# A second buffer for the keys of a head pair, loaded at an earlier place in the DMA queue

## The chip, the core and the metric

The kernel runs on one core of a Trainium2 chip. The metric is the device time in microseconds (us) of one execution, from its first to its last instruction and what lies around them. A core has a tensor engine (TensorE; PE in the profile, with its weight loads as PEld), a vector engine (DVE), a scalar engine (ACT), a GpSimd engine (POOL) and a sync engine (SP). Here SP computes nothing: nearly all DMA transfers are issued from its queue, in order, and an instruction that has to wait holds up all those behind it.

## The reference

Attention with queries that are averaged in pairs, for 8 batches of 8 heads, 1152 keys of 64 numbers, so 576 pooled queries per head; its output, put together as 576 rows of 512 per batch, goes through a token and channel mixing stage. All inputs and the output are float32.

```python
q_pool = q.reshape(B, H, S // 2, 2, D).mean(axis=3)
scores = scale * np.matmul(q_pool, k.transpose(0, 1, 3, 2))
attn = np.exp(scores - np.max(scores, axis=-1, keepdims=True))
attn = attn / (np.sum(attn, axis=-1, keepdims=True) + 1e-09)
x = np.matmul(attn, v)            # then (B, 576, 512)
theta = x @ w_theta
y = einsum('ts,bsd->btd', w_tok_r, x * cos(theta)) + einsum('ts,bsd->btd', w_tok_i, x * sin(theta))
u = x + y
out = u + np.maximum(u @ w_ch, 0.0)
```

## The kernel before

**Two stages.** The first computes the attention for 32 pairs of heads, one pair after the other; the second computes the mixing for the 8 batches. The change touches the first alone.

**Precision.** Each float32 operand of the scores is split into a rounded part `hi` and a rest `lo`, and a tile of scores is the sum of three products of these and of a fourth product that subtracts the maximum of each query (`escore`, L365). So before a pair's scores can start, its queries and keys must be transposed and split (`prep_t`, `prep_hi`, `prep_lo`), and the maxima of its scores must be known (`maxpass`, `max_tail`, `max_nm`). The maxima come as a tile with 9 rows (`mT`); four small DMAs bring them into one row per head (`load_max`, L358).

**The order.** The order is written out by hand: `plan(i)` (L643) puts every step of pair i at a position, 18 positions to a pair, position 18 i being the pair's first score tile. All steps of all pairs are sorted by position (L690) and issued in that order, and each engine and the DMA queue then goes through its own instructions in that order. In the stretch of a pair n (positions 18 n to 18 n + 18) lie

- the 18 score tiles of pair n (two halves of the queries, u = 0 and 1, with nine key blocks each), with the exponentials on ACT and the adds of the denominators on POOL (`ssum`, L387; 14 per pair);
- the 12 maxima passes of pair n + 2, one every position or two, each with two matmuls and a DVE reduction;
- at position 10.35 `burst(n, 0)`: the second part of the transposes of pair n + 2 (queries and the last three key blocks, `prep_t(n + 2, 1)`), the 36 matmuls with the values for u = 0 (`av`), and the transpose of the maxima of pair n + 1 into `mT`;
- at position 10.4 `load_max(n + 1)`, at 10.79 `load_k(n + 3)`, at 11 `load_v(n + 1)` and the store of the denominators, all on the queue of SP;
- at position 19.27, that is 1.27 positions into the next pair, `burst(n, 1)`: `tail_prep(n)` with the first part of the transposes of pair n + 3 (six key blocks, `prep_t(n + 3, 0)`) and the last maxima pass of pair n + 2, and then the `av` matmuls for u = 1.

So the keys of a pair are read twice: the first six blocks at the end of the pair three before it, the last three blocks nine positions later. The tile `kn` of a pair has one buffer (pool `inp`, `bufs=1`), and the load of the next pair's keys into it has to come after the second reading.

**Banks.** All TensorE results of this stage go in turn through four PSUM double banks (`bank2("e", ...)`, `PAIRS`): a tile can be written once the tile four before it has been read by ACT or DVE.

**Weights.** Beside the attention the weights of the second stage are loaded and split in pairs 0 to 17, one job to a pair, in small steps on DVE, POOL and ACT (`weights`, `W_SLOTS`): among them two DVE operations (L524, L528) after `burst(n, 1)`, then two POOL operations (L530, L532) that need them, and for the token weights five transposes on TensorE (L574, L581) just ahead of `burst(n, 0)`.

The lines that set the positions and issue the keys:

```python
at(base + pl["load_q"], 5, load_q, i)      # L646, base = 18 * i
at(base + pl["load_k"], 5, load_k, i)      # L648
kn = inp.tile([P, KT, 2, D], F32, tag="kn", name=f"kn{i}")                      # L226
nc.sync.dma_start(kn[:, :, h, :], k[b, h0 + h].rearrange("(p t) d -> p t d", t=KT))  # L228, h = 0, 1
```

Of the kernel before, what the change touches and what calls it, by code (L numbers as in the profile page):

```python
# [9 lines left out]
F32 = mybir.dt.float32  # L10
# [16 lines left out]
MAX_AT1 = (-18.123, -16.8, -16.1, -15.375, -14.7, -14.0, -13.3, -12.6, -11.714, -10.295, -9.8, -8.999)  # L27
PLAN = {
    "load_q": -44.542,
    "load_k": -43.209,  # L30
    "pool_q": -35.622,
    "load_max": -7.6,
    "load_v": -7.0,
# [41 lines left out]
def pooled_attention_moe_kernel(  # L75
# [12 lines left out]
    P = 128  # L88
    B, H, S, D = k.shape
# [5 lines left out]
    KT = S // P  # L95
# [94 lines left out]
    with ExitStack() as p1:  # L190
# [4 lines left out]
        inp = p1.enter_context(tc.tile_pool(name="inp", bufs=1))  # L195
# [16 lines left out]
        state = {}  # L212

        def load_q(i):
            b, hp = divmod(i, NP)
            h0 = 2 * hp
            qn = inp.tile([QP, 2, QT, 2, D], F32, tag="qn", name=f"qn{i}")
            nc.sync.dma_start(
                qn, q[b, h0 : h0 + 2].rearrange("h (p t f) d -> p h t f d", t=QT, f=2)
            )  # L220
            state[i] = dict(qn=qn)

        def load_k(i):
            b, hp = divmod(i, NP)
            h0 = 2 * hp
            kn = inp.tile([P, KT, 2, D], F32, tag="kn", name=f"kn{i}")  # L226
            for h in range(2):
                nc.sync.dma_start(kn[:, :, h, :], k[b, h0 + h].rearrange("(p t) d -> p t d", t=KT))  # L228
            state[i]["kn"] = kn

        def pool_q(i):
            qn = state[i]["qn"]
# [410 lines left out]
        def plan(i):  # L643
            base = NU * i
            pl = PLAN
            at(base + pl["load_q"], 5, load_q, i)  # L646
            at(base + pl["pool_q"], 5, pool_q, i)
            at(base + pl["load_k"], 5, load_k, i)  # L648
            if i < 3:
                at(PRO[i][0], 3, prep_all, i, 0)  # L650
            if i < 2:
                at(PRO[i][1], 3, prep_all, i, 1)
                at(PRO[i][2], 3, lambda i=i: (max_tail(i, None), max_tail_red(i)))
            if i == 0:
                at(-7.62, 3, first_row)
            at(base + pl["load_max"], 7, load_max, i)
            at(base + pl["load_v"], 5, load_v, i)
            gen = maxpass(i)
            for n in (MAX_AT0, MAX_AT1, MAX_AT)[min(i, 2)]:
                at(base + n, 2, run, gen, 1)  # L660
            at(base + pl["max_nm"], 7, max_nm, i)
            for u in range(2):
                for kt in range(KT):
                    at(base + KT * u + kt, 1, escore, i, u, kt)
                    at(base + KT * u + kt + (SS_LAG if i < NPAIR - 1 else 1.2), 8, ssum, i, u, kt)
            for u in range(2):
                at(base + AV_AT[u], 4, burst, i, u)
            for n, fn in (
                ("norm_spread", norm_spread),
                ("norm_store", norm_store),  # L670
            ):
                at(base + pl[n], 9, fn, i)
# [316 lines left out]
```

## Time and profile before

| | |
|---|---|
| median of 3 runs | 1400.39 us (1399.51 to 1400.64) |
| the profiled execution | 1399.06 us |
| its span, first to last instruction | 1397.3 us |
| first stage (32 pairs), until the tail of the last pair | about 888 us |
| TensorE busy | 1324.2 us (95%), mean granted clock 0.992 |
| POOL busy | 957.4 us (69%) |
| DVE busy | 817.3 us (58%) |
| ACT busy | 726.4 us (52%) |
| DMA | 111.64 MB, mean 80 GB/s |

The profile shows one execution. A line of the timeline gives the start, the duration, the engine and the line of the kernel, the operation with the tile it writes and those it reads, and in brackets how long the engine was idle before it and what ended that. Matmuls are pipelined: their starts are recorded, their ends are modelled. The waits sum, for each engine and line, the idle time and name the event that came last before its end. Busy times by windows are sums over all instructions of a stretch.

### The profile page before, as it was taken

To read this page: it belongs to the slowest core of one execution; us is meant where nothing else is said; L and a number is where in the kernel's file an instruction comes from. 1 tells how busy PE (TensorE), PEld (TensorE's weight loads), DVE (VectorE), ACT (ScalarE), POOL (GpSimd) and SP (SyncE) were. 2 spreads that over 40 slices of the span, in tenths; PEclk is the share of its full clock that TensorE was granted. 3 is DMA by queue.
4 is the path that set the end of the run, shared out by engine and by line. 5 is a ranking of instruction groups with operands and counts; after the bars stand their busy time and mean duration, and the time that the engine had idled before them with its cause. 6 is when DMAs were issued, how large, how long until landed. Compare 5 with 4: busy or idle time off the path is not lost.

```text
span 1397.3 us, 29769 instructions
## 1 busy us (share of the span) xinstructions
PE 1324.2 (95%) x12178; PEld 1081.9 (77%) x12178; DVE 817.3 (58%) x1056; ACT 726.4 (52%) x1272; POOL 957.4 (69%) x727
## 2 busy tenths in 40 slices
PE   5999999999999999999999999879999999999998
PEld 4667777777777777767677777579999999999998
DVE  5677777777776876555465552656354453536442
ACT  2556566566656656556555555544453444445431
POOL 2799999999999999788788788463452624345220
PEclk9999999999999999999999999889999999999999
DMA  5334343433433333233233223141212122121111
GB/s 125 101 93 114 98 110 88 115 96 101 125 88 109 86 89 86 65 92 87 61 96 86 61 62 99 34 143 47 60 54 75 54 68 69 47 60 54 27 32 37
DMA packets 123992, 111.64 MB, mean 80 GB/s; under 512 B 88128, under 2 KB 88512, under 8 KB 123856
## 3 DMA queue, kind: packets, MB, share of 16 engines
q1 hardware_dynamic: 123680, 109.28, 28.1%
q8 instruction: 96, 1.57, 0.5%
q0 software_dynamic: 176, 0.46, 0.1%
q14 instruction: 40, 0.33, 0.1%
HBM read 88.29 MB, written 21.27 MB: 78 GB/s over the span
## 4 chain that ended last, share of the span: by engine, by line
PE 76%; DMA 9%; DVE 5%; ACT 4%; issue 2%; POOL 2%; SPq 1%; POOLq 0%; ACTq 0%; DVEq 0%
PE pa L403 20%; PE pe L382 17%; PE py L820 12%; DMA kn<-in_k_dram 8%; PE pth L748 7%; PE pr L859 6%; PE pt L267 4%; PE pm L307 3%; PE pn L424 2%; DVE mx L314 2%; PE pxn L736 1%; PE px L324 1%; POOL ss L394 1%; ACT pc L385 1%; ACT xh L724 1%
## 5 line engine op out<-in xcount | busy, mean ns | idle before, releaser
L394 POOL TENSOR_TENSOR ss<-ss,pc 128x576 f32<-128x576 f32 x384 | 552.9, 1440 | 85.7 <-ACT pc L385 61.5
L314 DVE TENSOR_REDUCE mx<-pm 128x2 f32<-128x768 f32 x384 | 355.5, 956 | 182.3 <-PE pm L307 181.7
L385 ACT ACTIVATE pc<-pe 128x576 f32<-128x576 f32 x576 | 353.9, 652 | 63.3 <-PE pe L382 42.8
L403 PE MATMUL pa<-pc,vn 128*64 128x288 f32 x2304 | 293.5, 409 | 0.0
L820 PE MATMUL py<-wtk,Z 128*128 128x288 f32 x1728 | 244.0, 298 | 6.9 <-DVE r L765 6.9
L403 PEld LDWEIGHTS pa<-pc,vn 128*64 128x64 f32 x2304 | 159.5, 137 | 109.5 <-issue 3.3
L820 PEld LDWEIGHTS py<-wtk,Z 128*128 128x128 f32 x1728 | 235.0, 190 | 8.7 <-DVE r L765 7.3
L795 POOL TENSOR_TENSOR Z<-ab,Z 128x512 fp32r<-128x512 f32 x40 | 52.1, 1302 | 269.5 <-ACT Z L791 220.3
L382 PE MATMUL pe<-hi 64*128 64x288 f32 x1152 | 198.1, 340 | 1.8 <-DVE mx L314 0.7
L382 PE MATMUL pe<-lo,hi 64*128 64x288 f32 x1152 | 170.4, 292 | 0.0
L382 PE MATMUL pe<-hi,lo 64*128 64x288 f32 x1152 | 170.2, 292 | 0.0
L382 PE MATMUL pe<-nmr,oner 64*128 64x288 f32 x1152 | 170.2, 292 | 0.0
L382 PEld LDWEIGHTS pe<-hi 64*128 64x128 f32 x1152 | 108.1, 184 | 58.2 <-issue 23.1
L307 PE MATMUL pm<-hi 64*128 64x384 f32 x768 | 134.1, 347 | 3.9 <-ACT hi L283 2.1
L413 ACT COPY xu<-pa 128x288 f32<-128x288 f32 x64 | 25.6, 400 | 166.9 <-PE pa L403 123.9
L382 PEld LDWEIGHTS pe<-lo,hi 64*128 64x128 f32 x1152 | 109.1, 186 | 0.0
L382 PEld LDWEIGHTS pe<-nmr,oner 64*128 64x128 f32 x1152 | 108.6, 185 | 0.0
L382 PEld LDWEIGHTS pe<-hi,lo 64*128 64x128 f32 x1152 | 108.6, 185 | 0.0
L859 PEld LDWEIGHTS pr<-us,wch 128*128 128x128 f32 x768 | 104.4, 188 | 2.1
L859 PE MATMUL pr<-us,wch 128*128 128x288 f32 x768 | 105.9, 296 | 0.0
L294 DVE TENSOR_TENSOR lo<-pt,hi 128x768 fp32r<-128x768 f32 x64 | 67.4, 1053 | 48.5 <-ACT hi L283 48.5
L394 POOL TENSOR_TENSOR ss<-pc,pc 128x576 f32<-128x576 f32 x64 | 93.4, 1460 | 3.4 <-ACT pc L385 3.4
(108 smaller groups left out, 1700.4 us busy)
## 6 DMA issues: line engine op xcount, KB each, us to landing
qn<-in_q_dram SPq DMA_DIRECT2D x32, 576.0 KB
kn<-in_k_dram SPq DMA_DIRECT2D x64, 288.0 KB
vn<-in_v_dram SPq DMA_DIRECT2D x32, 576.0 KB
xd<-xu SPq DMA_DIRECT2D x32, 288.0 KB
xT<-xd SPq DMA_DIRECT2D x8, 1152.0 KB
dn<-rd SPq DMA_DIRECT2D x64, 144.0 KB
out_dram<-on SPq DMA_DIRECT2D x23, 192.0 KB
out_dram<-on SPq DMA_DIRECT2D x23, 128.0 KB
```

The lines of the kernel that those rows point to most:

```text
L267: nc.tensor.transpose(out=pt[:, n, c : c + R], in_=src.rearrange("p h d -> p (h d)"), identity=ident[0:R, 0:R],)
L294: nc.vector.tensor_tensor(lo, src, hi.bitcast(F32), ALU.subtract)
L307: nc.tensor.matmul(pm[:, h, 0:W], hi[hs, Q0 + j * P : Q0 + (j + 1) * P], hi[hs, K0[3 * g] : K0[3 * g] + W], start=True, stop=True,)
L314: nc.vector.tensor_reduce(mx[:, j : j + 5 : 4, g : g + 1], pm[:, :, 0:W], AX.X, ALU.max)
L382: nc.tensor.matmul(pe[:, h, 0:HALF], w[hs], x[hs], start=(n == 0), stop=(n == 3))
L385: nc.scalar.activation(pcs[u, kt], pe[:, :, 0:HALF], AF.Exp, scale=SC)
L394: nc.gpsimd.tensor_tensor(st["ss", u], first, st["pc"][u, kt], ALU.add)
L403: nc.tensor.matmul(pa[hs, 0, 0:HALF], st["vn"][:, h, kt, :], st["pc"][u, kt][:, h, :], start=(kt == 0), stop=(kt == KT - 1),)
L748: nc.tensor.matmul(th, xs[:, c, j * P : (j + 1) * P], ws[:, c], start=(n == 0), stop=(n == 11))
L795: engine("zlo", b).tensor_tensor(Z[1], t, Z[0].bitcast(F32), ALU.subtract)
L820: nc.tensor.matmul(st["py", c, u][:, 0:HALF], Z[zi][:, c * P : (c + 1) * P], wtk[wi][:, kw, u * HALF : (u + 1) * HALF], start=(i == 0 and ...
L859: nc.tensor.matmul(pr[u][:, 0:HALF], wch[wi][:, c, e * P : (e + 1) * P], st["us", ui][:, c, u * HALF : (u + 1) * HALF], start=(n == 0), st ...
```

## The change

The load of a pair's keys moves from position 18 i - 43.209 to 18 i - 53.5. Seen from the pair n in whose stretch it falls, `load_k(n + 3)` is issued at position 0.5, after the first score tile of pair n, in place of position 10.79 after `load_max(n + 1)`. The tile `kn` gets two buffers, which is 4608 bytes more in each partition. As `load_k` of a pair now comes ahead of its `load_q`, both put their tile into the pair's state without making it anew.

```diff
 PLAN = {
     "load_q": -44.542,
-    "load_k": -43.209,
+    "load_k": -53.5,
     "pool_q": -35.622,
     "load_max": -7.6,
     "load_v": -7.0,
@@ load_q
-            state[i] = dict(qn=qn)
+            state.setdefault(i, {})["qn"] = qn
@@ load_k
-            kn = inp.tile([P, KT, 2, D], F32, tag="kn", name=f"kn{i}")
+            kn = inp.tile([P, KT, 2, D], F32, tag="kn", name=f"kn{i}", bufs=2)
             for h in range(2):
                 nc.sync.dma_start(kn[:, :, h, :], k[b, h0 + h].rearrange("(p t) d -> p t d", t=KT))
-            state[i]["kn"] = kn
+            state.setdefault(i, {})["kn"] = kn
```

## Rows read from the trace of the kernel before

**Rows 1.** Waits of TensorE, whole span: engine, line, waited for: us, times, longest
```profile
PE pt L267 <- DMA kn<-in_k_dram: 33.2, 25, 7.8
...
PE pt L267 <- DVE mx L314: 4.1, 4, 1.1
...
PE pt L267 <- issue: 0.6, 1, 0.6
```

**Rows 2.** Windows: length, busy PE, PEld, DVE, ACT, POOL, clock, DMA share, GB/s
```profile
59.83:545.15 485.32, 466.03 (x5020) 348.45 (x5022) 356.21 (x401) 295.24 (x530) 450.88 (x332) 1.00 0.37 101
545.15:834.98 289.83, 280.21 (x3032) 208.86 (x3032) 162.93 (x190) 162.04 (x286) 236.07 (x175) 1.00 0.28 77
```

**Rows 3.** Timeline of TensorE, end of one pair and middle of the next
```profile
191.36 0.33 PE L307 MATMUL pm<-hi 64*128 64x384 f32 x2
192.40 0.85 PE L267 MATMUL pt<-ident,kn 128*128 128x128 f32 x6 [0.71 <-DMA kn<-in_k_dram]
193.00 0.71 PE L324 MATMUL px<-hi,tail 128*128 128x512 f32 x3
...
204.62 0.34 PE L307 MATMUL pm<-hi 64*128 64x384 f32 x2
204.89 0.71 PE L267 MATMUL pt<-ident,qp 96*128 96x96 f32 x6
```

**Rows 4.** Timeline of the queue of SP in the same pair
```profile
186.81 0.55 SPq L363 DMA_DIRECT2D nmr<-mT  x1
187.46 1.40 SPq L228 DMA_DIRECT2D kn<-in_k_dram  x2
...
190.82 1.16 SPq L497 DMA_DIRECT2D raw<-in_moe_w_tok_r_dram  x2
198.76 0.34 SPq L479 DMA_DIRECT2D xd<-xu  x1
```

**Rows 5.** Timelines of TensorE and DVE at the ends of two other pairs
```profile
327.75 0.84 PE L267 MATMUL pt<-ident,kn 128*128 128x128 f32 x6 [1.03 <-DVE mx L314]
...
649.12 0.85 PE L267 MATMUL pt<-ident,kn 128*128 128x128 f32 x6 [0.59 <-DMA kn<-in_k_dram]
...
648.57 0.96 DVE L314 TENSOR_REDUCE mx<-pm 128x2 f32<-128x768 f32 x1 [0.32 <-PE pm L307]
```

**Rows 6.** Timelines of DVE and ACT, end of the pair of Rows 3
```profile
189.60 1.82 DVE L314 TENSOR_REDUCE mx<-pm 128x2 f32<-128x768 f32 x2 [0.27 <-PE pm L307]
...
191.12 1.19 ACT L385 ACTIVATE pc<-pe 128x576 f32<-128x576 f32 x2 [0.16 <-PE pe L382]
```

**Rows 7.** Waits of POOL, from 59.83 to 545.15, then from 545.15 to 834.98
```profile
POOL raw L530 <- DVE raw L528: 12.8, 18, 1.6
POOL ss L394 <- ACT pc L385: 6.1, 10, 0.8
...
POOL ss L394 <- ACT pc L385: 46.0, 22, 3.0
```

**Rows 8.** Timelines of POOL and TensorE, a pair with token weights
```profile
119.22 1.47 POOL L532 TENSOR_TENSOR ws<-wf,raw 128x576 f32<-128x576 f32 x1
...
123.98 0.66 PE L574 MATMUL pwt<-ident,ws 128*128 128x128 f32 x4
```

**Rows 9.** Lines L524 and L528 on DVE: count, ns min/median/max, first and last start
```profile
L524 DVE SCALAR_TENSOR_TENSOR wf<-raw,wf x18: 680/942/1997, 62.0 to 520.4; 128x512 uint32<-128x512 uint32 x8, 128x576 uint32<-128x576 uint32 x8, 64x576 uint32<-64x576 uint32 x2
...
L528 DVE TENSOR_SCALAR raw<-wf x18: 428/1516/1553, 62.7 to 521.3; 128x512 uint32<-128x512 uint32 x8, 128x576 uint32<-128x576 uint32 x8, 64x576 uint32<-64x576 uint32 x2
```

**Rows 10.** Timelines of SP, DVE and TensorE, first microseconds
```profile
0.75 0.38 SPq L218 DMA_DIRECT2D qn<-in_q_dram  x1
1.20 1.45 SPq L228 DMA_DIRECT2D kn<-in_k_dram  x2
...
5.38 1.02 DVE L236 TENSOR_TENSOR qp<-qn 96x384 f32<-96x384 f32 x2 [4.41 <-DMA qn<-in_q_dram]
...
7.83 1.51 PE L267 MATMUL pt<-ident,kn 128*128 128x128 f32 x6 [7.83 <-DMA kn<-in_k_dram]
```

## The prediction

> **What bounds the kernel now.** I read the waits of TensorE first. Over the whole span it has 30 waits ahead of the first transposes of a pair's keys (L267): 25 are put down to the load of `kn`, 4 to a DVE reduction and 1 to nothing, 33.2 + 4.1 + 0.6 = 37.9 us [rows 1]. The longest, 7.8 us, is the start of the kernel [rows 10]; the other 29 are one for each pair whose end prepares a later one, 30.1 us, 1.04 us each. Nothing else of weight holds TensorE in this stage: from 59.83 to 834.98 it is busy for 466.03 of 485.32 us and 280.21 of 289.83 us, so idle for 19.3 and 9.6 us, whatever the cause [rows 2], and those 29 waits, less the first, are that. So the stage is bound by TensorE and one gap to a pair.
>
> The four waits put down to DVE are the same thing. At 327.75 the transposes start after 1.03 us, like their neighbours; at 649.12 they start while the last reduction, 648.57 to 649.53, still runs [rows 5]. That reduction is therefore not what they need, and its end beside the start at 327.75 is a coincidence.
>
> Why the keys are late is in the DMA queue: their two issues at 187.46 stand right behind the last maxima row (186.81), which waits for the middle of the pair, and the transposes start at 192.40, 4.9 us after the first issue [rows 3, 4]. TensorE comes to them at about 191.6.
>
> **The change, part by part.** *The wait.* Where no load is awaited, a transpose starts 0.27 us after the start of the last maxima matmuls (204.62, 204.89); at the end of the pair it starts 1.04 us after them (191.36, 192.40) [rows 3]. So 0.77 us go where the wait says 0.71, as the modelled end of the matmul overlaps what would follow. For 29 pairs that is 30.1 + 29 x 0.06 = 31.9 us. All of it lies on the path, since TensorE has no other idle time to take it up.
>
> *The new place in the queue.* The two issues (1.40 us) now come after the first score of pair n. Of SP's queue they pass the four maxima rows, the query load, a weight store in some pairs and the store of `xd`. They come to stand between the weight load (190.82 to 191.98) and that store (198.76) [rows 4]. SP stands idle between these for 6.8 us, so 1.40 us there delay nothing, and the value load behind the maxima rows goes out 1.40 us earlier. Were the cover gone, the store would slip by 1.40 us, and nobody on TensorE's path reads it. The transfer took 4.9 us with the value load behind it; behind a weight load I give it up to 8. It is wanted one pair after 192.40, and a pair takes about 27 us (485.3 us for 18, [rows 2]), so about 19 us are to spare.
>
> *The added wait.* The second buffer comes free with the last three key blocks of the pair two before, whose transposes lie just after the middle of the preceding pair: a pair before 204.89, so at about 178.5 [rows 3], 13 us ahead of the new issue. Behind a load that did wait there would be the store of `xd`, the queries and the maxima rows; I cost it at nothing.
>
> *What is late next on TensorE.* The transposes need the bank of the tile four before, the second reduction of a pair of them that ends at 191.42 (189.60 + 1.82), 0.2 us before TensorE would come at 191.63; the last maxima pass (`px`, 0.60 us after the transposes) needs an exponential that ends at about 191.7, half of 191.12 to 192.31, and would come at 192.23 [rows 3, 6]. Both are in time, the first by little: a cost between 0 and, at 0.1 us a pair, 2.9 us. I take 0, the row's own end.
>
> *POOL.* This is the cover that matters. In the pairs with weight work (59.83 to 545.15) POOL waits 12.8 us for DVE's L528 and 6.1 us for exponentials, together 18.9 us in 485.3 [rows 7]; TensorE would save up to 19.3 us there [rows 2]. The two come out level, so POOL has no time left in these 18 pairs. After 545.15 it waits 46.0 us while TensorE saves 9.6: ample [rows 2, 7]. A POOL that falls behind costs nothing until something on TensorE meets it. The nearest such thing is the token weights: POOL's L532 ends at 120.69, the transposes of its result start at 123.98, 3.3 us later [rows 8]. Bounds: if POOL can use all 18.9 us, it falls behind by 0.4 us overall and by 1 to 3 us (an estimate) after a pair or two with a long wait, and costs 0. If the 12.8 us can't be used, it falls behind by 19.3 - 6.1 = 13.2 us, and 13.2 - 3.3 = 9.9 us come back as waits. I take 1.3 us, near the lower end, since a wait is time in which POOL only stood.
>
> L528, the operation that POOL waits for, takes from 428 to 1553 ns, and L524 from 680 to 1997 [rows 9]: their spread is far more than their three sizes explain. The Trainium skill, "SBUF — State Buffer", section "Who interferes with whom", says that a VectorE instruction with two SBUF inputs or in a two-port mode and a GpSimd instruction that reads SBUF exclude each other, the later one blocked until the first is done. The spread in this trace agrees. By that rule a POOL add moved into today's waits would meet those two operations, the waits would come back as blocked time, and the sum would be the one with 9.9 us lost; it is the first rival.
>
> *The start.* Pair 0 now loads its keys ahead of its queries, and the keys of pair 1 follow at once. Today the queries are there at 5.38 and the keys at 7.83, 1152 KB after the first issues at 0.75 and 1.20 [rows 10]. Then the queries are the last, at about 7.8; their sums take 1.02 us on DVE, while the key transposes (1.3 us) are already done. That is 0.4 us better to, if the next 576 KB share the engines evenly at the 174 KB/us of these rows, 2.9 us worse. I take +0.2 us, as the queries that were issued first also landed first.
>
> *The sum.* From the profiled 1399.06 us: - 31.9 + 0.2 + 1.3 = - 30.4, so 1368.7. The median of the runs lies 1.3 us above the profiled one, which gives **1370.0 us**. The second stage starts after the last pair's sums and moves with them.
>
> **The rivals.** *POOL takes TensorE's place in the weight pairs.* For it: the level sums above, and the spread of L528. Against it: POOL's wait is idle time, and the lag has 3.3 us to grow. Time: 1399.06 - 31.9 + 0.2 + 9.9 + 1.3 = 1378.6.
>
> *Another wait takes the place of the load's,* at the bank or at the exponentials. For it: the margin of 0.2 us. Against: both are read to be in time. Were half the gap to stay, 16 us would be gained, 1384.
>
> *It doesn't do what it says:* the load is held in SP's queue until its old place. Against it: the buffer is free 13 us earlier. It would give the old time, 1399 to 1401.
>
> *Slower: POOL is displaced by DVE throughout.* A denser TensorE lets L524 and L528 always fall on POOL's adds, for their full medians, 0.94 + 1.52 = 2.46 us a pair, 44 us in 18 pairs [rows 9]. POOL would then need 485.3 - 18.9 + 44 = 510.7 us for the weight pairs, 25.4 more than they take now. Less the 9.6 us of the later pairs, and 2 of the pair before 59.83, it ends near 1414. It turns slower from a displacement of (18.9 + 9.6 + 2) / 18 = 1.7 us a pair. Against it: part of the 2.46 us is in today's times already, as the medians show.
>
> **How the numbers follow.** Chances: the forecast, 1366 to 1375, 0.66; POOL in TensorE's place, 1375 to 1385, 0.20; another wait, 1380 to 1395, 0.05; no effect 0.04; slower 0.05. The low end is 1366: no loss to POOL, 0.4 us won at the start, and some 2 us for waits that the trace puts elsewhere. The high end is 1381: the 1378.6 of the first rival with most of the start's 2.9 us. A difference under 0.2% (2.8 us) can't be told from none by a measurement of this kernel. Faster has the first three cases and comes to 0.91, same 0.04, slower 0.05.
>
> **What the profile after would show.** If the steps hold: the waits of L267 for `kn` are down to the one at the start; the two issues of `kn` stand between a weight load and the store of `xd`; TensorE is busy over 99% of the stretch of the pairs; POOL's waits in the weight pairs are nearly gone, those in the later pairs are down by some 10 us. The first rival would show waits of TensorE for POOL (at L574) or of ACT for buffers that POOL holds, and weight pairs longer by half a microsecond than their TensorE work. The second would show waits of L267 or L324 for DVE or ACT near 0.5 us. The prediction is wrong if the waits for `kn` go and the pairs still don't get shorter by about a microsecond.

## The result and the profile after

The changed kernel takes 1377.17 us (median of 4 runs, 1376.94 to 1378.85), against 1400.52 us for the kernel before beside it: a ratio of 0.9828 [0.9808, 0.9847], so faster by 1.7%. The measured gain is 23 us, where 30 were forecast (1370.0). The range of 1366 to 1381 holds the time, but only by the part that it has from the first rival: the time lies 2 us above the forecast's own case (1366 to 1375) and within 1.5 us of that rival's 1378.6.

The profiled run of the changed kernel took 1378.85 us (span 1377.1), 1.7 us above its median; that of the kernel before took 1399.06, 1.3 us below its median. The rows add up to the 20.2 us between these two.

**The waits of TensorE.** First those of the whole span, against [rows 1]; the columns are those of [rows 1].

```profile
PE pt L267 <- DMA kn<-in_k_dram: 7.2, 1, 7.2
...
PE pm L307 <- ACT pc L385: 5.1, 7, 0.8
...
PE pt L267 <- DVE qp L236: 2.5, 1, 2.5
```

Of the 30 waits for the keys one is left, that of the first pair. Two waits are new: 7 of the maxima matmuls for ACT's exponentials, all in the pairs with weight work, and one for the first pair's queries.

**Stretches of the same work.** I cut both profiles at the starts of the first key transposes at pair ends, as what lies between two such starts is the same work in both. Windows of the kernel before, then of the changed one: the 18 pairs with weight work, and the pairs after them up to the last such transposes. The columns are those of [rows 2].

```profile
58.46:543.77 485.31, 466.02 (x5018) 348.45 (x5019) 356.21 (x400) 295.24 (x530) 450.87 (x331) 1.00 0.37 101
543.77:808.72 264.95, 255.32 (x2761) 190.45 (x2761) 148.18 (x172) 147.29 (x260) 216.33 (x162) 1.00 0.30 80
```

```profile
57.08:529.92 472.84, 466.43 (x5020) 348.28 (x5019) 369.15 (x400) 296.79 (x531) 456.24 (x332) 1.00 0.41 105
529.92:785.37 255.45, 255.22 (x2762) 190.39 (x2760) 148.18 (x172) 147.19 (x261) 217.19 (x162) 1.00 0.31 83
```

The later pairs lose all their idle time: 264.95 to 255.45, beside 255.22 of TensorE's work. The pairs with weight work don't: 485.31 to 472.84, with 6.4 us of TensorE's time (472.84 - 466.43) still idle. All in all the gain is 2.8 us between the transposes of pair 0 (35.59 to 58.46 before, 37.01 to 57.08 now), 12.5 us, 9.5 us, less 1.4 us that the start takes longer (35.59 to 37.01), less 3.1 us in what follows the last transposes (588.6 before, 591.7 now).

**POOL and ACT in the pairs with weight work.** Waits of POOL in the changed kernel, from 57.08 to 529.92, and after the "..." from 529.92 to 785.37; then those of ACT for POOL in the first of these stretches.

```profile
POOL raw L530 <- DVE raw L528: 0.4, 1, 0.4
...
POOL ss L394 <- ACT pc L385: 30.1, 11, 3.3
```

```profile
ACT hl L541 <- POOL ws L532: 3.1, 4, 0.9
ACT wth L541 <- POOL ws L532: 2.8, 3, 0.9
ACT ws L514 <- POOL hl L543: 0.9, 4, 0.2
ACT ws L514 <- POOL wth L543: 0.6, 3, 0.2
```

POOL's 18.9 us of waits [rows 7] are down to 0.4: it is the engine that is full now. Who meets it is ACT, at the copy of a square weight (L541), 7 times for 5.9 us. ACT's exponentials are queued behind that copy, and TensorE waits for those: 7 times, 5.1 us. The timelines of POOL, ACT and TensorE show one such place, in the changed kernel:

```profile
170.32 1.31 POOL L532 TENSOR_TENSOR ws<-wf,raw 128x512 f32<-128x512 f32 x1
...
171.66 0.62 ACT L541 CAST wth<-ws 128x512 fp32r<-128x512 f32 x1 [0.92 <-POOL ws L532]
...
172.88 0.44 PE L307 MATMUL pm<-hi 64*128 64x384 f32 x2 [0.81 <-ACT pc L385]
```

The same step in the kernel before, in the pair with the least to spare:

```profile
199.81 1.31 POOL L532 TENSOR_TENSOR ws<-wf,raw 128x512 f32<-128x512 f32 x1
...
201.69 0.61 ACT L541 CAST hl<-ws 128x512 fp32r<-128x512 f32 x1
```

There POOL is done at 201.12 (199.81 + 1.31) and ACT comes at 201.69. ACT had no wait, but it had only 0.57 us to spare, and no row of waits shows a margin. At the other seven places where ACT makes this copy the margin before was 0.99 to 2.08 us.

**The queue.** The timeline of SP's queue shows the load where the prediction put it, between a weight load and the store of `xd`, with free time on both sides (in this pair a load of `rc` goes just ahead of it):

```profile
158.44 0.38 SPq L497 DMA_DIRECT2D raw<-in_moe_w_ch_dram  x1
161.22 0.34 SPq L161 DMA_DIRECT2D rc<-sd  x1
161.66 1.39 SPq L228 DMA_DIRECT2D kn<-in_k_dram  x2
167.70 0.33 SPq L479 DMA_DIRECT2D xd<-xu  x1
```

**The start.** First microseconds of the changed kernel, timelines of SP, DVE and TensorE:

```profile
0.76 1.48 SPq L228 DMA_DIRECT2D kn<-in_k_dram  x2
2.28 1.18 SPq L218 DMA_DIRECT2D qn<-in_q_dram  x1
3.50 1.96 SPq L228 DMA_DIRECT2D kn<-in_k_dram  x2
...
10.21 1.02 DVE L236 TENSOR_TENSOR qp<-qn 96x384 f32<-96x384 f32 x2 [9.24 <-DMA qn<-in_q_dram]
11.29 1.22 PE L267 MATMUL pt<-ident,qp 96*128 96x96 f32 x6 [2.54 <-DVE qp L236]
```

The queries of pair 0, issued second now, are there at 10.21 and not at 5.38 [rows 10], with the keys of the next pair issued behind them. This varies: in the four other profiled runs with these two buffers and this order they are there at 8.92 to 9.63.

### The profile page after: what moved, and what is told of

Same layout as the page of the kernel before. It is cut to its first block, busy times and chain, and to the rows that moved or that the text cites. A ratio compares the mean times of both kernels' runs of the same rounds, so it can differ in the third digit from the quotient of the medians.

```text
span 1377.1 us, 29805 instructions
## 1 busy us (share of the span) xinstructions
PE 1325.8 (96%) x12178; PEld 1081.0 (78%) x12178; DVE 830.6 (60%) x1056; ACT 727.7 (53%) x1272; POOL 961.5 (70%) x727
## 4 chain that ended last, share of the span: by engine, by line
PE 84%; DVE 5%; ACT 5%; POOL 3%; issue 2%; DMA 1%; SPq 0%; POOLq 0%; ACTq 0%; DVEq 0%
PE pe L382 23%; PE pa L403 20%; PE py L820 13%; PE pth L748 8%; PE pr L859 6%; PE pm L307 4%; PE pt L267 4%; PE pn L424 2%; DVE mx L314 1%; PE pxn L736 1%; POOL ss L394 1%; PE px L324 1%; ACT pc L385 1%; ACT xh L724 1%; PE po L882 1%
## 5 line engine op out<-in xcount | busy, mean ns | idle before, releaser
L394 POOL TENSOR_TENSOR ss<-ss,pc 128x576 f32<-128x576 f32 x384 | 560.2, 1459 | 68.2 <-ACT pc L385 42.0
L748 PE MATMUL pth<-wth,xh 128*128 128x512 f32 x320 | 93.4, 414 | 0.0
```

The lines of the kernel that those rows point to most:

```text
L394: nc.gpsimd.tensor_tensor(st["ss", u], first, st["pc"][u, kt], ALU.add)
L748: nc.tensor.matmul(th, xs[:, c, j * P : (j + 1) * P], ws[:, c], start=(n == 0), stop=(n == 11))
```

## The experiments

**Which half of the change does it?** The theory was that the place ahead of the maxima rows brings the gain and that the buffer only permits it. Two kernels take one half each, and a third has one buffer at another early place.

The second buffer alone, with the load at its old place:

```diff
-    "load_k": -53.5,
+    "load_k": -43.209,
```

> The second buffer alone: the keys are loaded at their old position 10.79, behind the maxima rows. Theory (the gain comes from the place in the queue, not from the buffer): the load is still held behind the maxima rows, so TensorE waits for the keys in 29 pairs as before, some 30 us, and the time is that of the kernel before, 1400 us, within 2 us. Rival (the single buffer held the load back, so that the second one is what gains): a gain of 10 us or more.

Measured: 1400.07 us, a ratio of 0.9986 [0.9970, 1.0002]. The waits of TensorE, whole span:

```profile
PE pt L267 <- DMA kn<-in_k_dram: 39.1, 29, 7.8
```

The waits are all there. The buffer by itself is worth nothing, since the keys were late by their place in the queue.

The new place alone, with one buffer:

```diff
-            kn = inp.tile([P, KT, 2, D], F32, tag="kn", name=f"kn{i}", bufs=2)
+            kn = inp.tile([P, KT, 2, D], F32, tag="kn", name=f"kn{i}")
```

> The new place alone, with the single buffer: the load stands at position 0.5 of SP's queue and waits there for the transposes at 10.35 of the same pair. Theory (place, not buffer, brings the gain, and the added wait costs only what stands behind it in the queue): the keys' issue falls just after those transposes, some 5 us ahead of the maxima rows and some 12 us ahead of its use, so the 29 waits for the keys go as in the changed kernel; the store of x and the loads of queries and weights behind it go out up to 13 us later, which has spare time for the queries: 1375 to 1382 us. Rival (the held queue makes something else late: weight loads, the maxima rows or the queries): TensorE waits elsewhere, 1385 to 1410 us.

Measured: 1390.20 us, 0.9922 [0.9904, 0.9940], 12.9 us above a second measurement of the changed kernel on the same chip (1377.27, below). The pairs are as in the changed kernel; the loss is at the start, where the first transposes of a pair end come at 41.76 us (35.59 before) and those of pair 0's end at 70.35 (57.08 in the changed kernel). The waits of TensorE and of SP's queue, whole span:

```profile
PE pm L307 <- ACT hi L283: 6.9, 3, 4.8
...
PE pe L382 <- DMA nmr<-mT: 4.9, 1, 4.9
```

```profile
SPq L228 <- PE pt L267: 470.1, 31, 16.8
```

The load now waits in the queue for the transposes that free its only buffer, about 15 us each time. In a pair SP has that time. At the start it hasn't: the first maxima rows are queued behind the load (issued from 31.23, 25.89 before). So the rival's cause was real, and the time lies in its range, but it acts at the start alone and not in every pair; the 29 waits for the keys went, as the theory said.

One buffer, and the load right behind the transposes that free it, so that nothing is held up in the queue (an edit of the kernel before):

```diff
-    "load_k": -43.209,
+    "load_k": -43.645,
```

> One buffer, the load at position 10.355: just behind the transposes that free it, ahead of the maxima rows, with nothing held in the queue; the first loads stay in their old order. Theory (the wait of the old place was for the maxima rows ahead of it alone): the issue falls some 5 us earlier than in the kernel before, the keys land some 4 us ahead of their use, all 29 waits go, and the time is that of the changed kernel less what that loses at the start, 1374 to 1376 us. Rival (the key transfer now lies ahead of the maxima rows on the DMA engines and makes them late): TensorE waits at the first scores of a pair, 1385 us or more.

Measured: 1378.21 us, 0.9832 [0.9818, 0.9847]; the pairs with weight work take 472.6 us. The waits of TensorE, and the first maxima row in the timelines of SP and TensorE:

```profile
PE pt L267 <- DMA kn<-in_k_dram: 7.8, 1, 7.8
```

```profile
28.44 1.31 SPq L228 DMA_DIRECT2D kn<-in_k_dram  x2
29.81 1.22 SPq L362 DMA_DIRECT2D nmr<-mT  x1
...
33.60 0.95 PE L382 MATMUL pe<-nmr,oner 64*128 64x288 f32 x2 [2.73 <-DMA nmr<-mT]
```

The 29 waits go with one buffer as well. The time came out 2 us over what was expected, as the keys of pair 2 go out just ahead of the first maxima row, for which TensorE stands 2.73 us; the first transposes of a pair end come at 39.86 us, 2.85 later than in the changed kernel. So the gain belongs to the place in the queue, ahead of the maxima rows, and the second buffer isn't needed for it.

**The changed kernel again,** for comparison on the chip of the second group:

> The changed kernel once more, as the measure for the runs beside it on the same chip: 1377 us, within 3 us, 0.983 of the kernel before.

Measured: 1377.27 us, 0.9824 [0.9806, 0.9842]; pairs with weight work 472.45 us. The result repeats, the missing part in those pairs too.

**Where is the rest of the gain in the weight pairs?** Theory A: POOL is full, and its lag meets ACT at the copy L541. Rival: another thing makes these pairs long, or the place of the copy alone. Three edits of the changed kernel.

The rest of a square weight (L543) is computed on DVE and not on POOL, 8 operations:

```diff
-                    yield from split_slow(hl[0], hl[1], ws[:, 0:DM], nc.gpsimd)
+                    yield from split_slow(hl[0], hl[1], ws[:, 0:DM], nc.vector)
...
-                    yield from split_slow(dst[0][:, c], dst[1][:, c], ws[:, 0:DM], nc.gpsimd)
+                    yield from split_slow(dst[0][:, c], dst[1][:, c], ws[:, 0:DM], nc.vector)
```

> The changed kernel with the last step of the square weight jobs (L543, 1.3 us on POOL in 8 pairs) on DVE. Theory A (POOL, full to the brim in the pairs with square weights, holds up ACT at L541 and so TensorE): those pairs go from 26.7 us towards the 25.5 us of TensorE's own work, 6 to 8 us less in all, 1369 to 1371 us. Rival B (these pairs are long because of what ACT or DVE have to do there, and POOL is only near): no gain, or a loss of up to 3 us, since DVE has 8 more operations: 1377 to 1380 us.

Measured: 1372.40 us, 0.9798 [0.9776, 0.9820], a gain of 4 to 5 us over the changed kernel by the medians (across chips), 1 to 3 less than expected; the weight pairs themselves are 2.8 us shorter (472.84 to 470.04). Its weight pairs in the windows, POOL's wait there, and the new operation in the timeline of DVE:

```profile
56.14:526.18 470.04, 468.09 (x5020) 348.48 (x5018) 371.45 (x408) 296.19 (x531) 447.78 (x324) 1.00 0.41 105
```

```profile
POOL raw L530 <- DVE raw L528: 5.4, 14, 0.4
```

```profile
196.84 1.01 DVE L543 TENSOR_TENSOR hl<-ws,hl 128x512 fp32r<-128x512 f32 x1
...
197.77 1.81 DVE L314 TENSOR_REDUCE mx<-pm 128x2 f32<-128x768 f32 x2
```

ACT's waits at L541 are gone, POOL has waits again, and TensorE's idle time falls from 6.4 to 2.0 us. But its own busy time is 1.7 us longer. The operation stands right in front of the maxima reductions that TensorE needs, which fits a part that is paid back there; that it is the cause was not tested by itself.

The copy L541 comes later, ahead of the next step that needs it:

```diff
-..., (5.0, "G"), (5.5, "S"), (7.0, "G"), ...
+..., (5.0, "G"), (6.9, "S"), (7.0, "G"), ...
```

> The changed kernel with ACT's copy of a square weight (L541) at position 6.9 instead of 5.5 of the pair; POOL has as much to do as in the changed kernel. Theory A (it is the place where POOL's lag is met: ACT's copy stands behind POOL's L532 and ahead of the exponentials): POOL has 1.4 positions, some 1.7 us, more before ACT wants its result, the waits of ACT at L541 (5.9 us) and of TensorE behind them (5.1 us) go, and the time falls by 5 to 8 us, to 1369 to 1372 us. Rival C (POOL is the bound of the weight pairs wherever it is met): its lag is met at another place, the gain is under 2 us, 1375 to 1377 us.

Measured: 1375.67 us, 0.9809 [0.9791, 0.9827], weight pairs 471.3 us. Waits of ACT for POOL and of TensorE, from 56 to 528:

```profile
ACT ws L514 <- POOL hl L543: 2.7, 4, 0.8
ACT ws L514 <- POOL wth L543: 2.3, 3, 0.8
ACT hl L541 <- POOL ws L532: 1.6, 3, 0.5
```

```profile
PE pe L382 <- ACT pc L385: 6.0, 8, 1.0
```

The waits at L541 shrink (from 5.9 us to 2.1, with 0.5 for `wth`), those at ACT's next meeting with POOL (L514) grow, and TensorE waits as long as it did, on another line. So the form of theory A in which the place of the copy is at fault fell: with POOL full, another place is only another meeting point.

The sums of the queries of pairs 3 to 19, which POOL computed in the weight pairs (two operations of about 1 us a pair), are computed on DVE:

```diff
-            eng = nc.vector if i == 0 else nc.gpsimd
+            eng = nc.vector if i == 0 or 3 <= i <= 19 else nc.gpsimd
```

> The changed kernel with the sums of the query halves (L236) of pairs 3 to 19 on DVE instead of POOL: 2 us less for POOL in each pair with weight work, some 1.1 us more for DVE. Theory A (POOL is what the weight pairs wait for): POOL waits again (for L528 and for exponentials), ACT's waits at L541 are gone, the 18 pairs fall from 472.8 us towards the 466 us of TensorE's own work, 4 to 6 us gained beside the changed kernel, 1371 to 1373 us. Rival B (ACT's copy of the square weights in the middle of the exponentials costs the time by itself): ACT's waits at L541 go, but the pairs with square weights stay at 26 us or more, and under 2 us are gained.

Measured: 1370.16 us, 0.9776 [0.9761, 0.9790], 7.1 us under the changed kernel beside it, where 4 to 6 were expected; the weight pairs give 5.5 of them, and the rest lies behind the last transposes (see "The sum" below). Its weight pairs, and the waits of POOL there:

```profile
56.91:523.89 466.98, 465.03 (x5021) 348.37 (x5019) 381.48 (x434) 295.71 (x531) 427.55 (x299) 1.00 0.42 106
```

```profile
POOL raw L530 <- DVE raw L528: 21.8, 18, 1.5
```

With POOL's busy time down from 456.24 to 427.55 us the weight pairs take 466.98 us against 472.45, TensorE is idle for 2.0 us in them, and ACT waits for POOL nowhere at L541. A pair with a square weight takes 25.7 us, where 7 of the 8 in the changed kernel take 26.4 to 26.8: the copy costs TensorE next to nothing when POOL is in time. DVE, which has more to do than before (381.48 us, 369.15 in the changed kernel), isn't it. It is POOL's load that holds these pairs.

The control, the same edit in the kernel before:

> The kernel before with the sums of the query halves of pairs 3 to 19 on DVE: the control to the same step in the changed kernel. Theory A (POOL becomes what the weight pairs wait for only once the waits for the keys are gone): TensorE still waits for the keys in 29 pairs, POOL only waits longer, and the time is that of the kernel before within 2 us. Rival (that step is a gain of its own, whatever TensorE waits for): 5 to 7 us gained here too.

Measured: 1402.59 us, 1.0002 [0.9985, 1.0019]. The waits of TensorE, whole span:

```profile
PE pt L267 <- DMA kn<-in_k_dram: 34.1, 27, 7.6
```

While TensorE waits for the keys, relieving POOL gives nothing. So POOL's bound came up only when the wait for the keys went.

**The start.** The changed kernel with the loads of pairs 0 and 1 at their old places:

```diff
-            at(base + pl["load_k"], 5, load_k, i)
+            at(base + (pl["load_k"] if i > 1 else -43.209), 5, load_k, i)
```

> The changed kernel with the keys of the first two pairs at their old positions, so that the queries of pair 0 are loaded first again. Theory (the start lost because the queries now come after the keys and share the DMA engines with the keys of pair 1): the maxima passes of pair 0 start at 13.1 us again instead of 15.3, and 1.4 to 2.2 us are gained, 1375 to 1376 us. Rival (the start is covered by what follows in pair 0): under 0.5 us.

Measured: 1374.66 us, 0.9802 [0.9784, 0.9821], some 2.5 us under the changed kernel by the medians (across chips). Timeline of DVE:

```profile
5.28 1.02 DVE L236 TENSOR_TENSOR qp<-qn 96x384 f32<-96x384 f32 x2 [4.31 <-DMA qn<-in_q_dram]
```

The queries are back at 5.28 and the first transposes of a pair end at 35.56, 1.45 us earlier; the pairs up to the last transposes take 728.0 us against 728.3. So about 1.4 us of the change's price are its order at the start, with a spread: these transposes come at 36.04 to 37.22 in the five profiled runs with the new order and two buffers, at 34.71 to 35.86 in the six with the first loads as before. The other microsecond by the medians lies behind the last transposes (589.6 us here, 591.7 in the changed kernel), where the granted clock differs from run to run (see "The sum" below).

**Both repairs together,** the changed kernel with this edit and that of the query sums:

> The changed kernel with the sums of the query halves of pairs 3 to 19 on DVE and the first two pairs' keys loaded at their old positions. If the two losses are separate, the 7.1 us of the first and the 1.4 us of the second add up: 1368 to 1370 us. If the gain at the start is covered, it is the time with the sums alone, 1370 to 1371 us.

Measured: 1368.16 us, 0.9752 [0.9733, 0.9771], weight pairs 466.97 us: the two losses are separate and add up. The same with one buffer, from the kernel before: the query sums on DVE, and the keys right behind the transposes, except for the first pairs:

```diff
-            at(base + pl["load_k"], 5, load_k, i)
+            at(base + (-43.645 if i > 2 else pl["load_k"]), 5, load_k, i)
```

> One buffer for the keys: from pair 3 on the load stands just behind the transposes that free it and ahead of the maxima rows, the first three pairs' keys are loaded as in the kernel before, and the sums of the query halves of pairs 3 to 19 are on DVE. Theory (the place alone brings the gain; with one buffer it lost only because the keys of pair 2 went ahead of the first maxima row): the time of the kernel with two buffers and both steps, 1368 to 1371 us. Rival (with one buffer the keys or the maxima rows come late in some pairs): 1373 us or more.

Measured: 1367.93 us, 0.9752 [0.9731, 0.9772]. Both beat the kernel before by 2.5% and the changed one by some 0.7%, and there is no difference between them: with POOL relieved and the start left in order, one buffer at the right place does what two do.

## Why the prediction was right or wrong

**The wait (-31.9): right.** All 29 waits went, and in the later pairs, where nothing else is short, 9.50 of the 9.6 us came (264.95 to 255.45). By the prediction's own sign, a pair shorter by about a microsecond, these 10 pairs have 0.95 us each and the 18 pairs with weight work 0.69. The reading that the four waits put down to DVE were waits for the keys held: they went with the others, while DVE's reductions stayed. That the stage had no second wait beside them held in e10: 466.98 us for weight pairs in which TensorE works for 465.03.

**POOL (+1.3): mis-sized, and this is the step that failed.** TensorE's idle time in the weight pairs was to fall by 19.3 - 1.3 = 18.0 us, and the stretch got shorter by 12.5; 5.5 us are missing, so the term that stood at 1.3 came to 6.8 (19.3 - 12.5). The bounds (0 to 9.9) held, the value in them did not. Two readings went wrong.

- *That a wait of POOL is time it can use.* Before, POOL needed 485.3 - 18.9 = 466.4 us by its rows, level with TensorE's 466.0. After, it needs 472.84 - 0.4 = 472.4. So 6.0 us came back, 5.4 of them as a longer busy time of POOL (450.87 to 456.24): about half of the 12.8 us in which POOL waited for L528, if the 6.1 us of its other waits could be used in full. Where they went, in the groups of POOL's and DVE's lines over the weight pairs (operation, count, busy time and mean ns of one), first before, then after:

```profile
L394 POOL TENSOR_TENSOR ss<-ss,pc 128x576 f32<-128x576 f32 x216 | 312.3, 1446 | 20.3 <-ACT pc L385 6.1
...
L528 DVE TENSOR_SCALAR raw<-wf 128x512 uint32<-128x512 uint32 (+2 forms) x18 | 20.0, 1111 | 0.6
```

```profile
L394 POOL TENSOR_TENSOR ss<-ss,pc 128x576 f32<-128x576 f32 x216 | 319.6, 1480 | 14.9
...
L528 DVE TENSOR_SCALAR raw<-wf 128x512 uint32<-128x512 uint32 (+2 forms) x18 | 27.7, 1537 | 0.6
```

  POOL's adds take 7.3 us more for the same count (their other form, L394 with two inputs `pc`, 2.1 us less), and DVE's L528 7.7 us more. The timelines of DVE and POOL show which adds: first a pair of the kernel before in which POOL waits, then a pair of the changed kernel.

```profile
144.38 0.46 DVE L528 TENSOR_SCALAR raw<-wf 128x576 uint32<-128x576 uint32 x1
144.92 1.15 POOL L530 TENSOR_TENSOR raw<-raw 128x576 f32<-128x576 f32 x1 [1.19 <-DVE raw L528]
```

```profile
164.89 1.51 DVE L524 SCALAR_TENSOR_TENSOR wf<-raw,wf 128x512 uint32<-128x512 uint32 x1
165.82 1.85 POOL L394 TENSOR_TENSOR ss<-ss,pc 128x576 f32<-128x576 f32 x1
166.44 1.52 DVE L528 TENSOR_SCALAR raw<-wf 128x512 uint32<-128x512 uint32 x1
```

  In the changed kernel an add lies across both DVE operations in each of the 18 pairs and takes 1885 ns in the mean; before, it did so in 11 pairs, at 1847. The adds that meet neither take 1435 in both kernels. That makes 18 x 0.45 - 11 x 0.41 = 3.6 of the 5.4 us. The prediction had the first rival's mechanism in hand (the spread of [rows 9], and the rule of the Trainium skill, "SBUF — State Buffer", section "Who interferes with whom") and gave it the smaller weight. The trace of after agrees with that rule: L528 now takes 1514 to 1559 ns every time, where the mean before was 1111, and it ends 0.29 to 0.32 us after the add that it meets. But it wasn't all or nothing, as the two bounds had it.

- *Where the lag is met.* The prediction named L574 as the nearest place, with 3.3 us [rows 8], and looked for places where TensorE reads POOL's result. The nearest one was a step further off: ACT reads POOL's L532 at L541, 0.57 to 2.08 us after it is done, and what ACT does next is what TensorE needs. With so much less to spare than 3.3 us, the lag is paid for in every pair that has a square weight but the first. The place itself counts for little, though: with the copy moved away (e5) the weight pairs are 1.5 us shorter (472.84 to 471.31). The text on what would show the rival had "ACT for buffers that POOL holds"; here it was ACT for a result of POOL.

The first rival was therefore right in kind (POOL in TensorE's place in the weight pairs), but not in its place, and its 9.9 us were too many: 6.4 us of TensorE's idle time stayed, 0.36 us a pair. That its time fits so well is in part luck: the start's 1.4 us and the 3.1 us behind the last transposes, neither in its sum at that size, make up for what it gave POOL too much.

**The start (+0.2): mis-sized.** It came to +1.4, in the bounds (-0.4 to +2.9). The queries, issued second, landed at 10.21, and at 8.92 to 9.63 in the other profiled runs with this order, where the prediction had them at about 7.8. Of these 3.5 to 4.8 us behind the old 5.38, 3.0 are the order itself: in e2, where the one buffer holds back the load behind them, they were there at 8.40. The other 0.5 to 1.8 us come with that load. e6 gives 1.45 us back.

**The rest: right where it said nothing is paid.** The load waits for no buffer (after the start SP stands ahead of it for at most 0.7 us, where e2 with one buffer has about 15), and the issues stand in SP's free time, as the queue above shows. The bank cost stayed at nothing: no wait of L267 for DVE is left but that for the first queries. POOL's waits in the later pairs fell by 11.5 us (41.6 to 30.1), against some 10. "TensorE over 99% busy" came true in the later pairs (255.22 of 255.45), not in the weight pairs (466.43 of 472.84, 98.6%).

**The sum.** Of the 10.1 us between the profiled 1378.85 and the 1368.7 that the sum gave, 5.5 are POOL's, 1.2 the start's, 0.3 small differences in the pairs, and 3.1 lie behind the last transposes. That last part is the run's own: it comes with the clock that TensorE was granted where the first stage ends and the second begins. The 60 us from the same point of the work, 74.5 us behind the start of the last key transposes, in the kernel before and in the changed one (columns of [rows 2]):

```profile
883.20:943.20 60.00, 47.60 (x260) 41.04 (x261) 32.13 (x43) 29.42 (x49) 29.48 (x23) 0.83 0.31 93
859.90:919.90 60.00, 47.53 (x243) 39.93 (x244) 34.02 (x44) 28.55 (x48) 28.96 (x22) 0.80 0.29 93
```

In the pairs, where TensorE was busy almost throughout, the granted clock was 1.00 in both. Here it was at the lower of its two levels (1.2 and 2.4 GHz) for part of the time, a little longer in this run of the changed kernel, and 17 matmuls fewer are recorded. The three profiled runs with 0.80 in this stretch take 591.5 to 592.5 us from the last transposes on, the ten with 0.83 to 0.86 take 588.4 to 589.6, and the changed kernel itself is on either side: its four runs took 1378.85 us at a mean clock of 0.990 and 1376.94 to 1377.31 at 0.992. What decides on the clock of a run stays open. In e12, with both repairs, the stretches up to the last transposes are 30.7 us shorter than in the kernel before (22.87 to 20.06, 485.31 to 466.97 and 264.95 to 255.38), so the wait was worth nearly the 31.9 us that the sum gave it.

## What to carry to other kernels

Before a stall of the bounding engine is taken away, add up what each other engine needs over the same stretch, and treat an engine that comes out level as full: its waits for a neighbour are only partly usable time when both work on the same memory. Then go through the places where any engine reads the level one's results, one or two steps away from the bounding engine too, and read from the timeline how much time is to spare at each; the smallest is where the lag shows first, and a table of waits doesn't show it. To move that place alone gains little while the engine stays full (e5); to take work off the engine gains what is left (e10). And ask of a second buffer whether it is the buffer or the place in the queue that was missing: here an earlier place with one buffer gave the same time.

## What the runs showed of the hardware

The same operation of DVE, L528 (128 x 512 to 576 elements), has a median of 1516 ns in the kernel before, 1548 in the changed one, where POOL has no time left, and 457 in the kernel with the query sums on DVE, where POOL waits for it 18 times:

```profile
L528 DVE TENSOR_SCALAR raw<-wf x18: 428/457/1553, 62.6 to 503.2; 128x512 uint32<-128x512 uint32 x8, 128x576 uint32<-128x576 uint32 x8, 64x576 uint32<-64x576 uint32 x2
```

The two lengths have no overlap, and what POOL does tells them apart: in all thirteen profiled runs (234 times in all) L528 takes 427 to 466 ns when POOL runs nothing, and 1510 to 1565 when an instruction of POOL runs as it starts, and then it ends 0.28 to 0.32 us after that instruction. So an operation's length can be a sign of what the other engine does at the time, and a short one beside a waiting engine isn't the price that it has when that engine works. The exchange isn't free in the other direction: in the kernel with the query sums on DVE these take 1754 ns in the median there, 992 on POOL, and POOL's adds are as long in the mean as in the changed kernel (1479 ns), as 49 of them now lie beside a query sum (1546 in the mean, 1440 for those that meet neither a query sum nor L524 or L528).
